# Two engines issue six blocks of a linear-attention and MLP kernel in the program's order, with smaller stages

## The chip, the cores and the metric

The kernel runs on one core of one Trainium2 chip. The metric is device time in microseconds (us). Three runs before the change took 1603.47, 1610.88 and 1611.52 us, median 1610.88. A profiled execution took 1603.45 us with a span of 1601.6 us from the first to the last instruction of the program, so 1.85 us lie around the span.

## The reference

```python
kv  = einsum('bhsd,bhse->bhde', k, v)        # 8 batches, 8 heads, 576 rows, 64 columns
out = einsum('bhsd,bhde->bhse', q, kv)
x   = out / sqrt(mean(out*out, -1) + 1e-6) * g_norm    # -> 4608 tokens x 512
h   = x @ w_in                               # 512 x 2048
g   = where(h >= 1, h, where(h <= -1, 0, (h + 1)**2 / 4))
x1  = g @ w_out                              # 2048 x 512
r   = maximum(x1 @ w_in2, 0)
out = (r * r) @ w_out2
```

The weights arrive as 64-bit floats, the rest as 32-bit floats.

## The kernel before

Every product of the two MLPs is made to single precision out of three fp32r matmuls: an operand is split into a high half (a cast, mostly on ScalarE) and a low half (a subtraction on VectorE), and high*high, high*low and low*high are added up in PSUM (`mm3`, L222). A weight is first narrowed from 64 bits (`narrow_w`, L250: one activation on ScalarE, L255, and two integer operations on VectorE, L257 and L258) and then split (`split_halves`, L168: cast and subtraction).

A *block* is 512 tokens through one MLP. `blocks` (L1001) lists seven plain blocks, those of batches 0 to 6 through the first MLP, that run one after the other. A block has 16 steps, one for each 128 columns of the hidden width; step `t` is one turn of the loop at L1098. A step has two halves. In the first half `h_stage` (L635) issues 12 matmuls into one of two PSUM banks (tag "h") and then a relu (ScalarE, L650), a square (ScalarE, L212) and a clamp that reads the bank again (VectorE, L652). In the second half `g_stage` splits the result (cast L204, subtraction L218) and `out_stage` issues the 12 matmuls of two steps earlier (`LAG = 2`) into four accumulators. After 16 steps the accumulators are copied out (L683 on VectorE, L685 on ScalarE) and stored.

Other work is hung into these halves by `hook(s, f, ...)` (L1004), where `s` counts half steps:

- Attention of batch `b` runs during block `b - 1`, four pairs of heads, one each 7 half steps (`attention`, L604). For a pair that starts at half step `s`: `kv_stage` and `t_stage` at `s` (the product of k and v, its copies `kvbd` at L462 and L463, the transpose of q at L522 and its split, L523 and L524), `o_stage` at `s + 2` and `s + 3`, `r_stage` at `s + 5` (the sum of squares, logarithm, exponential, a Newton step on VectorE, and the split of x).
- In block 0 the remaining 26 weight tiles of the first MLP are narrowed and split by `split_w` (L263), one each half step, three steps ahead of use. Loads of the raw weights are six steps ahead (L1012).
- In blocks 1 to 6 the weights of the later stages are prepared (L1026 to L1044): loads, narrowings, sums and splits, with stores from ScalarE's queue (`pay`, L162) to a scratch area in HBM.

After the plain blocks, five pairs of blocks go through a product with seven sub-products in place of eight (`in_phase`, `out_phase`), and a last plain block follows.

The order on each engine isn't that of this text: the framework's scheduler takes the instructions of each engine as they become ready by its own estimate of all durations, earlier ones of the program first, so an instruction can be put ahead of others that the program has earlier. The order it finds is then fixed; on the chip each engine follows it and waits where an operand isn't there.

Of the kernel before, what the change touches and what calls it, by code (L numbers as in the profile page):

```python
# [76 lines left out]
def linear_attention_rms_two_mlps(  # L77
# [19 lines left out]
    NF = DFF // P  # L97
    TB = 512
# [5 lines left out]
    AHEAD = 3  # L104
# [26 lines left out]
    LAST_B = B - 1  # L131
# [18 lines left out]
    def keep_halves(L, which, i, n, t):  # L150

        made = MADE[which][2 * n : 2 * n + 2]
        hs = slice(0, 2)
        if L == 1 and None in made and not (which == 1 and i + n * NH >= NF - TAIL):
            hs = slice(1, 2) if made[0] is None else slice(0, 1)
        owed.append(
            (wsd[L, which, i // 2][:, 2 * n + hs.start : 2 * n + hs.stop, i % 2], t[:, hs])
        )
# [3 lines left out]
    def pay(n):  # L162

        for dst, src in owed[:n]:
            nc.scalar.dma_start(dst, src)
        del owed[:n]

    def split_halves(t, src, hi, lo):  # L168

        src = src.rearrange("p (h f) -> p h f", h=2)  # L170
        copy(hi, t[:, :, 0, :], src)
        lo.tensor_tensor(t[:, :, 1, :], src, t[:, :, 0, :].bitcast(F32), ALU.subtract)  # L172
# [11 lines left out]
    engines = {"A": nc.scalar, "D": nc.vector, "P": nc.gpsimd}  # L184
# [6 lines left out]
    def engine(op, phase):  # L191
        return engines[next(turns[op][min(phase, 2)])]

    def scaled(e, dst, src, scale):
        if e is nc.scalar:
            e.activation(dst, src, AF.Copy, scale=scale)
        elif e is nc.vector:
            e.tensor_scalar_mul(dst, src, scale)
        else:
            e.tensor_scalar(dst, src, scale, 0.0, op0=ALU.mult, op1=ALU.add)  # L200

    def copy(e, dst, src):
        if e is nc.scalar:
            e.copy(dst, src)  # L204
        elif e is nc.vector:
            e.tensor_copy(dst, src)
        else:
            scaled(e, dst, src, 1.0)

    def square(e, dst, src):  # L210
        if e is nc.scalar:
            e.activation(dst, src, AF.Square)  # L212
        else:
            e.tensor_tensor(dst, src, src, ALU.mult)

    def split(t, src, op, phase):
        copy(engine(op + "_hi", phase), t[:, 0, :], src)
        engine(op + "_lo", phase).tensor_tensor(  # L218
            t[:, 1, :], src, t[:, 0, :].bitcast(F32), ALU.subtract
        )  # L220
# [26 lines left out]
    def d_tile(name, dtype=F32):  # L247
        return dt.tile([P, TB], dtype, tag=f"dt{next(d_tags)}", name=name)

    def narrow_w(L, f, which, phase):  # L250

        raw = w_raw.pop((L, f, which))
        low, high = raw[:, :, 0], raw[:, :, 1]
        as_float = high.bitcast(F32)
        nc.scalar.activation(as_float, as_float, AF.Prelu, scale=REBIAS, alpha=SIGN)  # L255
        t = d_tile(f"d{L}_{which}_{f}", I32)
        nc.vector.tensor_scalar(t, low, 29, None, op0=ALU.logical_shift_right)  # L257
        nc.vector.scalar_tensor_tensor(  # L258
            t, high, 3, t, op0=ALU.logical_shift_left, op1=ALU.bitwise_or
        )  # L260
        return t.bitcast(F32)

    def split_w(L, f, which):  # L263

        phase = int(f >= AHEAD)
        w = narrow_w(L, f, which, phase)
        dst = wi if which == 0 else wo
        t = wp.tile([P, 2, 2, H2], F32R, tag=f"w{which}_{f}", name=f"w{L}_{which}_{f}")
        split_halves(t, w, engine("w_hi", phase), engine("w_lo", phase))
        dst[L, f] = t  # L270
        if which == 1 and f >= NF - TAIL:
            keep_halves(L, which, f % NH, f // NH, t.bitcast(F32))
# [89 lines left out]
    xs = {}  # L362
# [4 lines left out]
    hl = {}  # L367
    og = {}
# [6 lines left out]
    def bank(b, name):  # L375

        pool, tag = next(banks) if b == 0 else (ps_t, "at")
        return pool.tile([P, TB], F32, tag=tag, name=name)
# [67 lines left out]
    def kv_stage(b, hp):  # L446
        kt, vt = kvm.pop((b, hp))
        r = kvr.pop((b, hp))
        ps = bank(b, f"pkv_{b}_{hp}")


        kv = ps[:, :P]
        for c in range(MR):
            nc.tensor.matmul(kv, kt[:, c], vt[:, :, c, :], start=c == 0, stop=False)
        nc.tensor.matmul(kv, r[0], r[1], start=False, stop=True)
        for j in range(2):
            s = slice(j * D, (j + 1) * D)
            if b == 0:
                copy(engine("kv_hi", b), kv0[s, hp, s], ps[s, s])
                continue  # L460
            t = kvbd[turn[b, hp] % len(kvbd)]
            copy(engine("kv_hi", b), t[s, 0, s], ps[s, s])  # L462
            nc.vector.tensor_tensor(t[s, 1, s], ps[s, s], t[s, 0, s].bitcast(F32), ALU.subtract)  # L463
# [54 lines left out]
    def t_stage(b, hp):  # L518
        work = [ap1.tile([P, S], F32, tag=f"wk{n}", name=f"wk{n}_{b}_{hp}") for n in range(2)]
        qT = ap1.tile([P, S], F32, tag="wk2", name=f"qf_{b}_{hp}")  # L520
        parts = [ap1.tile([P, S], F32R, tag=f"hl{n}", name=f"qT{n}_{b}_{hp}") for n in range(2)]
        nc.vector.transpose(qT, qs.pop((b, hp)))  # L522
        copy(engine("q_hi", b), parts[0], qT)  # L523
        engine("q_lo", b).tensor_tensor(parts[1], qT, parts[0].bitcast(F32), ALU.subtract)  # L524
        hl[b, hp] = (work, parts)
# [19 lines left out]
    def r_stage(b, hp):  # L545
        (y, o), _ = hl.pop((b, hp))
        s2 = og.pop((b, hp))
        ms = []
        for half in range(2):
            c = slice(half * U, (half + 1) * U)  # L550
            ps = bank(b, f"pr_{b}_{hp}_{half}")
            m = ps[:, :U]
            for n in range(2):
                nc.tensor.matmul(m, ones, s2[n][:, c], start=n == 0, stop=n == 1)
            nc.scalar.activation(y[:, c], m, AF.Ln, bias=lnb, scale=LN_SCALE)
            ms.append((c, m))
        nc.scalar.activation(y, y, AF.Exp, bias=expb, scale=-0.5)
        t = ap1.tile([P, S], F32, tag="wk2", name=f"t_{b}_{hp}")
        square(engine("y", b), t, y)
        for c, m in ms:  # L560
            newton(t[:, c], m)
        if b < LAST_B:
            norm(t, y, o)
            nc.gpsimd.tensor_copy(xrem[b][:, hp, :], t[:, TB:])
            split(xs[1, b][hp], t[:, :TB], "x", b)
            return
        xt = st.tile([P, TB], F32, tag="st", name=f"xt_{hp}")
        nc.vector.scalar_tensor_tensor(t, t, -3.0, y, op0=ALU.add, op1=ALU.mult)
        nc.vector.tensor_tensor(xt, o[:, :TB], t[:, :TB], ALU.mult)
        nc.vector.tensor_tensor(xrem[b][:, hp, :], o[:, TB:], t[:, TB:], ALU.mult)  # L570
        x_kept[hp] = xt

    x_kept = {}

# [29 lines left out]
    def attention(b, base, every, order):  # L604

        slots = []
        for j, hp in enumerate(order):
            s = base + every * j
            turn[b, hp] = len(turn)
            slots += [  # L610
                (max(0, s - 7), load_kv, b, hp),
                (max(0, s - 7), load_q, b, hp),
                (s, kv_stage, b, hp),
                (s, t_stage, b, hp),
                (s + 2, o_stage, b, hp, 0),
                (s + 3, o_stage, b, hp, 1),
            ]
            if j == 0:
                slots.append((s + 5, begin, b))
            slots.append((s + 5, r_stage, b, hp))  # L620
            if b == LAST_B:
                slots.append((s + 7, keep_x, b, hp))
        if b < LAST_B:
            slots.append((2 * NF * b, store_xrem, b))
        return slots
# [378 lines left out]
    def hook(s, f, *a):  # L1004
        hooks.setdefault((s // 2, s % 2), []).append((f, a))
# [8 lines left out]
            hook(2 * i + w, load_w, 1, i + 6, w)  # L1014
    for i in range(NF - AHEAD):
        for w in range(2):
            hook(2 * i + w, split_w, 1, i + AHEAD, w)
    for b in range(1, PLAIN):
        for f in range(NF - TAIL, NF):
            hook(2 * (b * NF + f - 1) + 1, load_tail, b, f)  # L1020
# [5 lines left out]
    for j in range(2 * NH):  # L1026
        which, i = j % 2, j // 2
# [43 lines left out]
    for j in range(2):  # L1071
        s = slice(j * D, (j + 1) * D)
# [22 lines left out]

    N1 = len(blocks) * NF
    step = lambda t: (*blocks[t // NF], t % NF)
    for t in range(N1):  # L1098
        h_stage(*step(t))
        n = len(owed)  # L1100
        for f, a in hooks.get((t, 0), []):
            f(*a)
        pay(n)
        n = len(owed)
        g_stage(*step(t))
        if t >= LAG:
            out_stage(*step(t - LAG))
        for f, a in hooks.get((t, 1), []):
            f(*a)
        pay(n)  # L1110

    late = []
    for n in range(NS):
# [16 lines left out]
    L, b = 2, NB - 1  # L1130
# [47 lines left out]
```

## Time and profile before

| | |
|---|---|
| median of three runs | 1610.88 us (1603.47 to 1611.52) |
| profiled execution, its span | 1603.45 us, 1601.6 us |
| TensorE busy | 1573.7 us, 98% of the span |
| VectorE, ScalarE, GpSimd busy | 1071.9, 943.7, 135.2 us |
| mean of the granted TensorE clock | 0.993 of full speed |
| moved by DMA | 355.55 MB, mean 222 GB/s |

Busy time of an engine is the time in which one of its instructions ran. What an idle stretch waited for is read from the views of waits, and in which stage it lies from the views of windows and of the order of time. In these, PE is TensorE, DVE is VectorE, ACT is ScalarE, SP is SyncE; a queue has a "q" behind its engine. L12 is line 12 of the kernel.

### The profile page before, as it was taken

Reading aid. Unit: us, or ns where it says so; the run is one execution under the profiler, and the core shown is the slowest. Engines: PE = TensorE matmul, PEld = TensorE weight load, DVE = VectorE, ACT = ScalarE, POOL = GpSimd, SP = SyncE. Lnnn points to the kernel's source line nnn. Section 1 sums busy time; section 2 is a strip of 40 time slices with the busy share of each in tenths; the row PEclk is TensorE's granted clock in tenths of the full one; section 3 lists DMA queues with packets and bytes.
Section 4 is the critical chain, followed back from the end, with each engine's and each line's share of the span. In section 5 each row is a group of like instructions: output and inputs, shape, how many; then the busy total and the mean of one; then the engine's idle time right before and its main releaser. Section 6 shows DMA issues by size and latency. Waiting matters only on the chain. (4 is left out here: it accounts for less than half of the span.)

```text
span 1601.6 us, 20867 instructions
## 1 busy us (share of the span) xinstructions
PE 1573.7 (98%) x7112; PEld 1295.6 (81%) x7112; DVE 1071.9 (67%) x1806; ACT 943.7 (59%) x1731; POOL 135.2 (8%) x117
## 2 busy tenths in 40 slices
PE   8999999999999999999999999999999999999998
PEld 5788888888878888788888888887788888888887
DVE  6887776877867787553487549776964496457522
ACT  5787666667666676664665466455646563664321
POOL 0000000000000000001310121012101300320000
PEclk9899999999999999999999999999999999999999
DMA  9897878796877978724676867696676677876783
GB/s 280 236 285 239 245 247 272 222 288 195 246 227 237 285 213 262 256 76 151 197 239 196 223 212 243 193 245 175 221 247 203 215 223 194 244 217 184 191 249 105
DMA packets 327513, 355.55 MB, mean 222 GB/s; under 512 B 196464, under 2 KB 221040, under 8 KB 327408
## 3 DMA queue, kind: packets, MB, share of 16 engines
q1 hardware_dynamic: 288496, 282.91, 61.7%
q10 hardware_dynamic: 38912, 71.31, 11.9%
q8 instruction: 57, 0.93, 0.2%
q14 instruction: 48, 0.39, 0.1%
HBM read 270.01 MB, written 84.15 MB: 221 GB/s over the span
## 5 line engine op out<-in xcount | busy, mean ns | idle before, releaser
L829 PE MATMUL po<-t,ws 128*128 128x512 f32 x1680 | 385.6, 391 | 3.3 <-DVE t L765 2.9
L829 PE MATMUL ph<-x,ws 128*128 128x512 f32 x1680 | 384.4, 391 | 2.3 <-DVE e L874 2.3
L829 PEld LDWEIGHTS po<-t,ws 128*128 128x128 f32 x1680 | 314.2, 188 | 74.0 <-DVE t L765 8.8
L829 PEld LDWEIGHTS ph<-x,ws 128*128 128x128 f32 x1680 | 316.4, 188 | 69.3 <-DVE e L874 3.6
L225 PE MATMUL ph<-x,w 128*128 128x512 f32 x1344 | 335.5, 394 | 5.8 <-ACT x L204 3.4
L225 PEld LDWEIGHTS ph<-x,w 128*128 128x128 f32 x1344 | 249.5, 189 | 58.1 <-ACT x L204 4.4
L765 DVE TENSOR_TENSOR t<-g,t 128x512 fp32r<-128x512 f32 x240 | 169.1, 710 | 80.6 <-ACT t L204 78.7
L204 ACT CAST t<-g 128x512 fp32r<-128x512 f32 x240 | 145.3, 621 | 89.5 <-DVE t L765 61.1
L225 PE MATMUL acc<-gs,w 128*128 128x512 f32 x696 | 172.6, 393 | 2.3 <-ACT ev L685 2.3
L225 PE MATMUL acc<-gs,wt 128*128 128x512 f32 x648 | 156.8, 391 | 0.0
L225 PEld LDWEIGHTS acc<-gs,w 128*128 128x128 f32 x696 | 128.7, 188 | 28.2 <-ACT ev L685 2.7
L225 PEld LDWEIGHTS acc<-gs,wt 128*128 128x128 f32 x648 | 120.4, 188 | 24.2
L650 ACT ACTIVATE u<-ph,halfb 128x512 f32<-128x512 f32 x112 | 77.1, 689 | 101.2 <-PE ph L225 100.2
L881 DVE TENSOR_TENSOR h<-ph,e 128x512 f32<-128x512 f32 x120 | 82.5, 690 | 61.8 <-PE ph L829 55.3
L652 DVE SCALAR_TENSOR_TENSOR u<-u,ph 128x512 f32<-128x512 f32 x112 | 76.5, 684 | 66.3 <-ACT u L212 65.5
L204 ACT CAST gs<-u 128x512 fp32r<-128x512 f32 x128 | 79.4, 621 | 57.0 <-DVE u L652 32.6
L895 POOL TENSOR_TENSOR t<-g 128x512 f32<-128x512 f32 x40 | 53.8, 1344 | 693.0 <-DVE h L881 284.3
L218 DVE TENSOR_TENSOR gs<-u,gs 128x512 fp32r<-128x512 f32 x128 | 87.8, 687 | 36.2 <-ACT gs L204 34.9
L888 ACT ACTIVATE h<-h 128x512 f32<-128x512 f32 x96 | 60.6, 631 | 57.3 <-DVE h L881 52.8
L874 DVE TENSOR_TENSOR e<-ph,e 128x512 f32<-128x512 f32 x80 | 54.1, 687 | 53.2 <-PE ph L829 52.3
L204 ACT CAST x<-xr 128x512 fp32r<-128x512 f32 x74 | 45.9, 621 | 49.4 <-DVE xr L797 35.1
L212 ACT ACTIVATE u<-u 128x512 f32<-128x512 f32 x112 | 70.6, 632 | 1.7 <-DVE s L172 1.1
(127 smaller groups left out, 1715.9 us busy)
## 6 DMA issues: line engine op xcount, KB each, us to landing
ws<-wsd SPq DMA_DIRECT2D x312, 512.0 KB, 4.0
wsd<-s ACTq DMA_DIRECT2D x96, 512.0 KB, 4.4
wt<-wsd SPq DMA_DIRECT2D x54, 512.0 KB, 4.9
raw<-in_moe_w_in_dram SPq DMA_DIRECT2D x32, 512.0 KB, 5.4
raw<-in_moe_w_out_dram SPq DMA_DIRECT2D x32, 512.0 KB, 5.3
xr<-x1d SPq DMA_DIRECT2D x36, 256.0 KB, 5.0
wsd<-w ACTq DMA_DIRECT2D x17, 512.0 KB, 4.6
k<-in_k_dram SPq DMA_DIRECT2D x32, 256.0 KB, 5.8
```

The costliest lines, as they stand in the source:

```text
L204: e.copy(dst, src)
L212: e.activation(dst, src, AF.Square)
L218: engine(op + "_lo", phase).tensor_tensor(t[:, 1, :], src, t[:, 0, :].bitcast(F32), ALU.subtract)
L225: nc.tensor.matmul(dst, wt(a), xt(c), start=first and n == 0, stop=last and n == 2)
L650: nc.scalar.activation(u, ps, AF.Relu, bias=halfb, scale=0.5)
L652: nc.vector.scalar_tensor_tensor(u, u, 1.0, ps, op0=ALU.min, op1=ALU.max)
L765: engine2(op + "_lo").tensor_tensor(t[:, 1, :], src, t[:, 0, :].bitcast(F32), ALU.subtract)
L829: nc.tensor.matmul(ps, wt(a), xt(c), start=first and n == 0 and i == 0, stop=last and n == len(lhs) - 1 and i == 2, skip_group_check=True,)
L874: nc.vector.tensor_tensor(e[i, p], bank, e[i, 1], ALU.add)
L881: nc.vector.tensor_tensor(h, bank, add, ALU.add)
L888: nc.scalar.activation(u, h, AF.Relu)
L895: engine2("t_sum").tensor_tensor(t1[k], b, a, ALU.subtract)
```

## The change

ScalarE (`Activation`) and VectorE (`DVE`) issue everything that the first 96 steps (blocks 0 to 5) emit in the order of the program. TensorE, GpSimd and SyncE stay with the scheduler, and so does where instructions emitted outside of the region fall among those inside. Block 6 and all that follows are as before.

Within the half steps, work is divided anew:

- The copies `kvbd` out of PSUM (`kv_copy`) and the split of q (`q_split`) come a half step after the product and the transpose.
- `r_stage` ends with the square at `s + 5`; the Newton step and the norm (`n_stage`) come at `s + 6`, the split of x (`x_stage`) at `s + 7`.
- `split_w` is divided: the narrowing stays at its half step, the split into halves comes one half step later. The six tiles made before step 0 are still done in one.

```diff
+    narrowed = {}
+
+    def first_half(L, f, which):
+        narrowed[L, f, which] = narrow_w(L, f, which, int(f >= AHEAD))
+
+    def second_half(L, f, which):
         phase = int(f >= AHEAD)
-        w = narrow_w(L, f, which, phase)
+        w = narrowed.pop((L, f, which))
         ...
@@ kv_stage
+        pkv[b, hp] = ps
+        if b == 0:
+            kv_copy(b, hp)
+
+    def kv_copy(b, hp):
+        ps = pkv.pop((b, hp))
         ...
@@ t_stage
         nc.vector.transpose(qT, qs.pop((b, hp)))
+        hl[b, hp] = (work, parts, qT)
+
+    def q_split(b, hp):
+        work, parts, qT = hl.pop((b, hp))
         copy(engine("q_hi", b), parts[0], qT)
         ...
@@ r_stage
         square(engine("y", b), t, y)
+        og[b, hp] = (y, o, t, ms)
+
+    def n_stage(b, hp):
+        y, o, t, ms = og[b, hp]
         for c, m in ms:
             newton(t[:, c], m)
         if b < LAST_B:
             norm(t, y, o)
             nc.gpsimd.tensor_copy(xrem[b][:, hp, :], t[:, TB:])
-            split(xs[1, b][hp], t[:, :TB], "x", b)
             return
         ...
+    def x_stage(b, hp):
+        t = og.pop((b, hp))[2]
+        if b < LAST_B:
+            split(xs[1, b][hp], t[:, :TB], "x", b)
@@ attention
                 (s, t_stage, b, hp),
+                (s + 1, kv_copy, b, hp),
+                (s + 1, q_split, b, hp),
                 ...
             slots.append((s + 5, r_stage, b, hp))
+            slots.append((s + 6, n_stage, b, hp))
+            slots.append((s + 7, x_stage, b, hp))
@@ hooks of block 0
-            hook(2 * i + w, split_w, 1, i + AHEAD, w)
+            hook(2 * i + w, first_half, 1, i + AHEAD, w)
+            hook(2 * i + w + 1, second_half, 1, i + AHEAD, w)
@@ main loop
-    for t in range(N1):
+    def one_step(t):
         h_stage(*step(t))
         ...
+    with tc.manual_schedule(engines={mybir.EngineType.Activation, mybir.EngineType.DVE}):
+        for t in range(N1 - NF):
+            one_step(t)
+    for t in range(N1 - NF, N1):
+        one_step(t)
```

## Rows read from the trace of the kernel before

**Rows 1.** The page: busy time by engine, and the granted clock in 40 slices.
```profile
PE 1573.7 (98%) x7112; PEld 1295.6 (81%) x7112; DVE 1071.9 (67%) x1806; ACT 943.7 (59%) x1731; POOL 135.2 (8%) x117
...
PEclk9899999999999999999999999999999999999999
```

**Rows 2.** Waits of TensorE, whole span: who waited for whom; us, times, longest.
```profile
PE ph L225 <- ACT x L204: 3.4, 2, 1.9
...
PE po L225 <- ACT qT L204: 2.8, 2, 2.0
...
PE acc L225 <- ACT ev L685: 2.3, 1, 2.3
...
PE ph L225 <- DVE x L218: 1.2, 1, 1.2
...
PE ph L225 <- DVE u L652: 1.1, 2, 0.8
PE po L225 <- ACT kvbd L204: 1.0, 1, 1.0
```

**Rows 3.** Windows of blocks 0 and 1: length, busy us (instructions) by engine, clock, DMA.
```profile
47.00:147.00 100.00, 98.93 (x467) 82.45 (x467) 86.57 (x159) 80.86 (x161) 1.88 (x4) 0.99 0.86 258
147.00:245.00 98.00, 98.00 (x469) 82.42 (x468) 74.00 (x139) 67.28 (x134) 1.81 (x4) 1.00 0.81 252
```

**Rows 4.** Order of time, VectorE then TensorE: start, us, what [idle before].
```profile
460.99 0.43 DVE L257 TENSOR_SCALAR d<-raw 128x512 int32<-128x512 int32 x1 [3.19 <-DMA raw<-in_moe_w_in_dram]
...
462.30 0.78 DVE L522 STREAM_TRANSPOSE qf<-q 128x576 f32<-128x576 f32 x1
...
463.84 0.40 PE L225 MATMUL po<-qT,kvbd 128*128 128x288 f32 x1 [2.04 <-ACT qT L204]
```

**Rows 5.** Waits of VectorE, 45 to 631 us.
```profile
DVE d L257 <- DMA raw<-in_moe_w_in_dram: 24.2, 10, 3.7
```

**Rows 6.** Order of time before step 0, ScalarE then VectorE.
```profile
40.61 0.62 ACT L204 CAST x<-t 128x512 fp32r<-128x512 f32 x1 [0.82 <-DVE t L494]
...
41.10 0.79 DVE L257 TENSOR_SCALAR d<-raw 128x512 int32<-128x512 int32 x2
41.81 1.28 DVE L258 SCALAR_TENSOR_TENSOR d<-raw,d 128x512 int32<-128x512 int32 x2
43.02 0.68 DVE L218 TENSOR_TENSOR x<-t,x 128x512 fp32r<-128x512 f32 x1
```

**Rows 7.** Groups of instructions: count | busy us, mean ns | idle before.
```profile
L650 ACT ACTIVATE u<-ph,halfb 128x512 f32<-128x512 f32 x112 | 77.1, 689 | 101.2 <-PE ph L225 100.2 <-DVE s L347 0.4
L652 DVE SCALAR_TENSOR_TENSOR u<-u,ph 128x512 f32<-128x512 f32 x112 | 76.5, 684 | 66.3 <-ACT u L212 65.5
L212 ACT ACTIVATE u<-u 128x512 f32<-128x512 f32 x112 | 70.6, 632 | 1.7 <-DVE s L172 1.1
...
L524 DVE TENSOR_TENSOR qT<-qf,qT 128x576 fp32r<-128x576 f32 x28 | 21.1, 752 | 2.0 <-ACT qT L204 2.0
...
L204 ACT CAST qT<-qf 128x576 fp32r<-128x576 f32 x28 | 18.8, 670 | 16.9 <-DVE qf L522 15.4 <-DMA wsd<-s 1.3
...
L463 DVE TENSOR_TENSOR kvbd<-pkv,kvbd 64x64 fp32r<-64x64 f32 x56 | 12.3, 219 | 9.2 <-ACT kvbd L204 8.0
```

**Rows 8.** Order of time, TensorE: 12 matmuls right behind those of `h_stage` of step 4.
```profile
63.81 2.89 PE L225 MATMUL acc<-gs,w 128*128 128x512 f32 x12
```

**Rows 9.** Order of time, SyncE's queue: a raw weight load.
```profile
61.29 0.37 SPq L237 DMA_DIRECT2D raw<-in_moe_w_in_dram  x1
```

**Rows 10.** DMA issues, 40 to 140 us: count, size, us to landing.
```profile
wsd<-w ACTq DMA_DIRECT2D x13, 512.0 KB, 4.1
raw<-in_moe_w_in_dram SPq DMA_DIRECT2D x12, 512.0 KB, 4.8
```

**Rows 11.** End of block 5: ScalarE in order of time, and a window.
```profile
646.55 0.58 ACT L685 COPY ev<-acc 128x512 f32<-128x512 f32 x1 [3.95 <-DMA x1d<-ev]
...
645.00:650.00 5.00, 2.81 (x8) 2.45 (x9) 0.69 (x1) 2.45 (x5) 0.00 (x0) 0.68 0.70 271
```

More of the change, by code (lines that the diff above doesn't have):

```diff
@@ L263, in split_w @@
     def split_w(L, f, which):
+        first_half(L, f, which)
+        second_half(L, f, which)
+    narrowed = {}
+    def first_half(L, f, which):
+        narrowed[L, f, which] = narrow_w(L, f, which, int(f >= AHEAD))
+    def second_half(L, f, which):
         phase = int(f >= AHEAD)
-        w = narrow_w(L, f, which, phase)
+        w = narrowed.pop((L, f, which))
         dst = wi if which == 0 else wo
@@ L455, in kv_stage @@
         nc.tensor.matmul(kv, r[0], r[1], start=False, stop=True)
+        pkv[b, hp] = ps
+        if b == 0:
+            kv_copy(b, hp)
+    pkv = {}
+    def kv_copy(b, hp):
+        ps = pkv.pop((b, hp))
         for j in range(2):
```

## Prediction

> **What bounds the kernel now.** I read the page first: TensorE is busy for 1573.7 of 1601.6 us, VectorE for 1071.9 and ScalarE for 943.7, and the granted clock is at nine tenths or more in every slice [rows 1]. So TensorE bounds it, and the change touches neither its instructions nor the work of another engine: it can win only what TensorE waits for, 27.9 us of idle time in the whole span and what the clock loses around it. The next view is that of TensorE's own waits, and the reader is to sort them by stage [rows 2]. The waits for x (3.4 from ScalarE, 1.2 from VectorE) lie before step 0. The 2.3 for an accumulator's copy lies at step 97, behind the region. Inside the region lie 2.8 for the split of q, 1.0 for the copies of the k-v product, and 1.1 for a clamp that frees a bank: 4.9 us in some 590. The windows say the same of whole blocks: block 0 leaves TensorE 1.07 us idle of 100, block 1 none of 98, while VectorE works 86.6 and 74.0 us in them, ScalarE 80.9 and 67.3 [rows 3]. There is little to win in the stage that changes, and both engines have room left.
>
> Why those few waits are there is read in order of time. At 460.99 VectorE starts a narrowing after 3.19 us of waiting for a raw weight to land; the transpose of q, at 462.30, stands behind it in the queue; the split of q follows, and TensorE waits 2.04 us for it at 463.84 [rows 4]. The narrowing was put ahead of attention by the scheduler because it reckoned the load to be there. VectorE waited so ten times, 24.2 us in all [rows 5].
>
> The Trainium skill ("TensorE: Matmul & The Clock Gate", section on the architectural detail of the array) says that the queues of ScalarE and VectorE are strictly first in, first out. The trace agrees in the rows just named: a ready transpose stood behind a load of 3.19 us. By that rule an order fixed by hand makes each wait hold all that the program has behind it, so it speaks against the change as much as for it; this is the slower rival below, priced there from rows.
>
> **The change part by part.**
>
> *Waits that go.* In the program's order a narrowing of the later weights comes five half steps behind its load, and the split of q one half step behind the transpose, so the pattern of rows 4 should not come up. The same holds for the copies of the k-v product, and for the clamp, which now stands right behind its square. I take all 4.9 us as gone; ends: none of it goes, 0, and all of it, -4.9. Late next is nothing that TensorE waits for in these places; the next limit is its own work.
>
> *The start.* The last part of x is cast by 40.61 + 0.62 = 41.2, but VectorE subtracts at 43.02, since two L257 and two L258 (0.79 + 1.28 = 2.07 us) run in between [rows 6]. The instructions of step 0 and later now wait behind the first relu, which needs x. Six tiles are made before step 0; I count seven narrowings begun by then, so one pair of the two is of a later tile: half of 2.07, -1.0. Ends: 0 (the scheduler puts another tile there) and -2.1. That tile's work comes back in block 0, where VectorE has 100 - 86.6 = 13 us free.
>
> *A step in order.* From the end of the 12 matmuls of `h_stage`: relu 0.69, square 0.63, clamp 0.68, 2.0 us in a row [rows 7]. TensorE wants that bank again after three groups of 12 matmuls, 3 x 2.89 = 8.7 us [rows 8]. So everything that stands in front of clamp or relu may be late by 6.7 us at no cost; beyond that TensorE pays all of it. The heaviest half step of block 0 has on VectorE the clamp 0.68, a narrowing (2.07 / 2 = 1.04), a tile's subtraction and the norm's two operations (all of the sizes of rows 7, 0.7 to 0.75), and two Newton steps of half width, an estimate of 0.45 each: 4.8 us against 2.89 of TensorE. It leaves 1.9 us of lateness, under 6.7. Cost 0; if the cover goes, 1.9 us for each of 24 pairs is the other end, and I hold it unlikely, since VectorE has 13 us free in a block and the next half steps are light.
>
> *The moved attention work.* Nothing is added: copies, splits and norms keep their instructions. But a half step's work on ScalarE and VectorE runs while TensorE is one half step ahead. In half of the pairs (12 of 24, those with an odd start) `kv_copy` and `q_split` fall into a first half, behind relu and square: 0.69 + 0.63, then two casts and two subtractions of 64x64 in turn (0.22 each, 0.9), then 0.67 and 0.75 for q, 3.6 us in all [rows 7]. TensorE reaches the product with q after one group, 2.89 [rows 8]: 0.7 late, at most 12 x 0.7 = 8.4 us if it stands there. At least 0: the scheduler still orders TensorE and can put the next 12 matmuls first. The nearest row is what TensorE waited for the same two things before, 2.8 + 1.0 us; I take +3.0. What is queued behind a late product is ScalarE's three evictions of it and the next relu, which have the 6.7 us. The Newton step, a half step later, holds the sum's bank longer; TensorE's product of the next pair needs it after a group of matmuls more, and is again the scheduler's to place. The other halves of moved steps (x, at `s + 7`) are needed a block later: 0.
>
> *Loads and stores.* A narrowing starts on ScalarE, so a late raw weight now holds ScalarE and VectorE together. Example in block 0: the load issued at 61.29 lands 4.8 us later, 66.1 [rows 9, 10]; step 4's matmuls end at 63.81, relu and square take it to 65.1, so ScalarE waits 1.0 us there [rows 7, 8]. Hidden in 6.7: 0. Ends: 0 and +24.2, all that VectorE waited on such loads before [rows 5]. SyncE's queue keeps its order by the scheduler, and its loads wait for earlier transfers to end. ScalarE's queue also issues the stores of halves. In 40 to 140 us it issues 13 whole ones, though block 0 has only nine tiles to store by the program; four came early [rows 10] and now go to their places in blocks 1 to 3. That takes 4 x 0.5 MB, about 8 us at 258 GB/s, out of a block where DMA is busy for 0.86, and puts it where it is 0.81 [rows 3]. Neither was on TensorE's path: 0, and if anything raw weights land earlier.
>
> *Behind the region.* At step 97 ScalarE waits 3.95 us to copy an accumulator, because the tile is still being stored; TensorE stops for 2.3, and the window at 645 to 650 shows a clock of 0.68, a stretch at 1.2 GHz in place of 2.4 [rows 2, 11]: 5 x 0.32 = 1.6 us more. Block 6 isn't in the region, so I leave it: 0, between -3.9 and +3.9 as transfers fall otherwise.
>
> *The sum.* 1603.45 - 4.9 - 1.0 + 3.0 = 1600.5 us, against the profiled execution. That execution stands at the lower of two levels of the runs (1603.5, and 1610.9 to 1611.5, 7.4 us up); the median is at the upper. I can't say at which the next median falls, 1600.5 or 1608, and predict 1604, between them.
>
> **The rivals.**
>
> *The stalls only move.* As many new waits come as go, 1603.5 (at the median's level 1611). For it: the old order had only 4.9 us of them, which is already what an order found by readiness can do. Against: the pattern of rows 4 has one cause, and the program's order takes it away.
>
> *Start and block 6 gain too.* All 4.9, the whole 2.1, and 3.9 at step 97 with no new waits: -10.9, 1592.5 (1600 at the median's level). For it: fewer stores in flight and less work pulled ahead. Against: nothing in the change orders step 97.
>
> *Loads at the head of both queues* (the other side). Where raw weights land late, the relu stands behind the narrowing on ScalarE and the clamp behind it on VectorE. It decides from the point at which a wait and the lateness at hand pass 6.7 us together: a load late by 4.8. If half of 24.2 us reaches TensorE, +12.1 on the sum, 1612.6 (1620 at the median's level). For it: SyncE's queue has little lead in block 0 [rows 9, 10] and ten such waits stood in the old order. Against: the longest of these waits was 3.7 [rows 5], and the narrowings now come later.
>
> **How the numbers follow.** The forecast (1600.5 at the profile's level) 0.45, stalls only move 0.12, start and block 6 gain 0.27 (with what the two levels of the runs give by chance), loads at the head 0.16. Over 0.5%, 8 us, is about what a measurement of this kernel can tell from no change: faster 0.27, within 0.57, slower 0.16. The range goes from 1591, just below the faster rival, to 1620, the slower one at the median's level.
>
> **What would show it.** In the profile after: TensorE's waits for the split of q, the copies and the clamp inside the first 630 us below 3 us in sum, and no wait of VectorE for raw weights in blocks 1 to 5; the subtraction of the last x a microsecond earlier behind its cast; VectorE's and ScalarE's busy time unchanged; 2.3 us at the copies of block 5's accumulators still there. Wrong would be: TensorE's waits above 10 us in the region, most of them on a clamp with ScalarE in front held by a load, or a gap long enough to bring a stretch at 1.2 GHz into blocks 1 to 5.

## The result, and the profile after

The changed kernel takes 1625.39 us (median of 4 runs, 1623.92 to 1625.85); the kernel before, run beside it, 1610.72 (1603.47 to 1611.52). The ratio is 1.010, 95% interval 1.007 to 1.0129: slower, with an interval clear of 1, and outside the range of 1591 to 1620. The profiled execution took 1625.6 us with a span of 1623.6, 22.0 us over the span before, where the medians differ by 14.7: the profiled execution of the kernel before was its fastest of four, and 22 executions of it beside later runs spread from 1601.05 us (mean granted clock 0.995) to 1616.00 (0.990). The 22.0 us below are those of this one pair of executions.

The page of the kernel after, busy time by engine and the granted clock in 40 slices:

```profile
PE 1581.6 (97%) x7111; PEld 1291.9 (80%) x7112; DVE 1080.7 (67%) x1806; ACT 950.5 (59%) x1731; POOL 138.3 (9%) x117
...
PEclk9899999999999999999999999999999999999999
```

Against [rows 1], ScalarE works 6.8 us more and VectorE 8.8 us more, both under 1%, so neither engine has become the bound. TensorE's idle time grew from 27.9 to 42.0 us, and its busy time by 7.9. What it waits for, whole span (who waited for whom; us, times, longest):

```profile
PE ph L225 <- DVE u L685: 13.1, 13, 1.8
PE ph L225 <- ACT x L204: 4.0, 2, 2.7
...
PE acc L225 <- ACT gs L204: 3.0, 1, 3.0
...
PE acc L225 <- DVE gs L218: 2.1, 2, 1.9
...
PE po L225 <- DVE qT L545: 0.3, 1, 0.3
```

The waits that the prediction set out to remove are gone: ScalarE's split of q and the copies of the k-v product, 3.8 us in [rows 2], are not in the list any more; the 0.3 for q's low half on VectorE stood before too. In their place stands the clamp (L685 after the change), 1.1 us before and 13.1 now. The windows of [rows 3] for the kernel after (length, busy us and instructions of TensorE, its weight loads, VectorE, ScalarE, GpSimd; clock, DMA share, GB/s):

```profile
47.00:147.00 100.00, 92.20 (x419) 73.15 (x419) 82.24 (x146) 76.33 (x149) 2.15 (x4) 0.98 0.76 230
147.00:245.00 98.00, 97.44 (x463) 81.26 (x462) 66.13 (x119) 64.35 (x126) 1.68 (x4) 1.00 0.69 210
```

Block 0's window holds 419 matmuls in place of 467. VectorE and ScalarE do less in it than before: they are late and idle at once. To place the loss I counted matmuls in the trace and compared when the last of the 12 matmuls of `out_stage` of a step ended. Microseconds by which a kernel is behind the one before, after step 0, block 0 (step 16), half of the region (48, 64), block 5's last steps (92), and the region (98). Each line is of one execution, and its kernel is told of below:

```
after step                          0     16     48     64     92     98
after                             1.6   10.3   17.7   20.0   16.5   23.5
order in blocks 1 to 5            0.0   -1.5    3.7    6.0    2.7    9.8
order in block 0                  2.1   16.7   18.2   18.8   16.8   13.7
order in blocks 0 to 4            2.0   11.0   17.4   19.7   25.8   21.9
casts first                       1.5    7.2   12.7   12.6    7.3   11.8
weights in four parts             1.7    9.2   14.2   16.5   13.6   20.1
both                              1.2    5.8   11.7   11.8    6.3    9.2
casts first, blocks 1 to 4        0.9   -0.5    6.4    6.3    4.0    1.7
less ScalarE work in block 0      3.2    7.7   13.4   15.7   13.1   19.9
less VectorE work in block 0      1.6    4.4   10.2   12.5    9.9   16.0
division alone, no order         -1.6   -2.9    3.5    5.1    3.4    2.5
division, casts first, no order   6.1    4.8    6.3    8.1    8.2    7.8
```

The last two lines are of kernels that are no slower by their medians, so a figure of the table can be off by several microseconds. It also holds what TensorE's own order moves: the scheduler puts a step's `out_stage` now earlier, now later among other work. By the products of `h_stage`, the kernel after is 2.8 us ahead after step 1, then 10.9 behind after step 16, 13.2 after 48, 16.3 after 64, 15.8 after 92 and 24.8 after 98. So it loses most, 13.7 us, in block 0; another 5.4 by step 64, nothing to 92, and 9.0 in steps 92 to 98. Now one stretch of block 0, all engines in order of time (start, us, what [idle before]):

```profile
72.29 2.92 PE L225 MATMUL acc<-gs,w 128*128 128x512 f32 x12
...
73.47 0.67 ACT L683 ACTIVATE u<-ph,halfb 128x512 f32<-128x512 f32 x1
73.62 0.78 DVE L539 STREAM_TRANSPOSE qf<-q 128x576 f32<-128x576 f32 x1
74.17 0.63 ACT L212 ACTIVATE u<-u 128x512 f32<-128x512 f32 x1
74.33 0.65 DVE L172 TENSOR_TENSOR w<-d,w 128x512 fp32r<-128x512 f32 x1
...
74.71 0.19 ACT L204 CAST kvbd<-pkv 64x64 fp32r<-64x64 f32 x1
74.90 0.41 DVE L257 TENSOR_SCALAR d<-raw 128x512 int32<-128x512 int32 x1
75.42 0.69 DVE L258 SCALAR_TENSOR_TENSOR d<-raw,d 128x512 int32<-128x512 int32 x1
76.03 0.68 DVE L685 SCALAR_TENSOR_TENSOR u<-u,ph 128x512 f32<-128x512 f32 x1
...
76.62 0.21 DVE L480 TENSOR_TENSOR kvbd<-pkv,kvbd 64x64 fp32r<-64x64 f32 x1
...
76.76 1.43 PE L225 MATMUL ph<-x,w 128*128 128x512 f32 x5 [1.55 <-DVE u L685]
76.86 0.21 ACT L204 CAST kvbd<-pkv 64x64 fp32r<-64x64 f32 x1 [1.97 <-DVE kvbd L480]
```

The reader is to follow three things. The square that the clamp reads ends at 74.80, yet the clamp starts at 76.03: VectorE has a transpose, a weight's low half and a narrowing ahead of it. TensorE is done at 75.21 and waits 1.55 us for that clamp. And ScalarE, after the first of its two casts of the k-v product, stands 1.97 us before the second: VectorE's first subtraction uses the same PSUM bank and the same tile `kvbd`, comes before the second cast in the program, and is itself behind the clamp. Until then neither the cast of q's high half nor any later relu can start. In this step ScalarE and VectorE each wait for what the other has queued.

ScalarE's waits in the region, 45 to 640 us, kernel after:

```profile
ACT kvbd L204 <- DVE kvbd L480: 41.5, 24, 3.5
ACT x L204 <- DVE t L511: 29.7, 21, 1.7
ACT s L558 <- PE po L225: 23.3, 12, 3.8
...
ACT u L683 <- PE ph L225: 3.7, 4, 1.4
```

and the same engine in the kernel before, 45 to 631 us:

```profile
ACT u L650 <- PE ph L225: 73.1, 58, 2.8
...
ACT kvbd L204 <- DVE kvbd L463: 2.9, 2, 2.5
```

Before, ScalarE stood ready for TensorE's next bank 58 times; after, 4 times. The wait between the two casts was 2.9 us in all before, and is 41.5 after. The relu of steps 2 to 5 started 0.0 to 1.1 us behind the end of its 12 matmuls before and 6.9 to 9.0 after; over steps 2 to 13 of block 0 it was 0.0 to 7.0 before and is 6.7 to 12.1 after. The Trainium skill ("PSUM — Partial Sum Buffer", section on terms, rows on the bank and the quadrant) says that two engines on the same bank and the same quadrant of 32 partitions at once are an error, and that different quadrants of a bank may be accessed at the same time. The two halves lie in partitions 0 to 63 and 64 to 127, so by that rule the second cast needn't wait for the first subtraction; the order that this framework gave made it wait 24 times, whether for the bank or for the tile `kvbd` that both write, and no run here tried the two at once.

### The profile page after: what moved, and what is told of

The parts are those of the page before. It is cut to its first block, busy times and chain, and to the rows that moved or that the text cites. A ratio compares the mean times of both kernels' runs of the same rounds, so it can differ in the third digit from the quotient of the medians.

```text
span 1623.6 us, 20967 instructions
## 1 busy us (share of the span) xinstructions
PE 1581.6 (97%) x7111; PEld 1291.9 (80%) x7112; DVE 1080.7 (67%) x1806; ACT 950.5 (59%) x1731; POOL 138.3 (9%) x117
## 5 line engine op out<-in xcount | busy, mean ns | idle before, releaser
L225 PE MATMUL ph<-x,w 128*128 128x512 f32 x1344 | 345.8, 398 | 17.5 <-DVE u L685 13.1
L225 PE MATMUL acc<-gs,wt 128*128 128x512 f32 x648 | 161.6, 393 | 4.9 <-ACT gs L204 3.0
L685 DVE SCALAR_TENSOR_TENSOR u<-u,ph 128x512 f32<-128x512 f32 x112 | 76.7, 685 | 56.6 <-ACT u L212 56.2
```

Source lines behind the costliest of these rows:

```text
L225: nc.tensor.matmul(dst, wt(a), xt(c), start=first and n == 0, stop=last and n == 2)
L685: nc.vector.scalar_tensor_tensor(u, u, 1.0, ps, op0=ALU.min, op1=ALU.max)
```

## The experiments

Theory 1: the order on both engines costs the 22 us, the division nothing. Rivals: the division does it; or one engine's order alone does.

**The division alone.**

```diff
-    with tc.manual_schedule(engines={mybir.EngineType.Activation, mybir.EngineType.DVE}):
-        for t in range(N1 - NF):
-            one_step(t)
-    for t in range(N1 - NF, N1):
+    for t in range(N1):
         one_step(t)
```

> The stages are divided as in the changed kernel, but the scheduler orders ScalarE and VectorE again. Theory 1 (the fixed order makes the two engines wait for each other at the heads of their queues, and the division is harmless): the 22 us of the profiled executions go, span 1598 to 1606 us, TensorE's waits for the clamp in block 0 under 2 us. Rival (the half-step-later hand-overs themselves make clamp and splits late): span 1615 us or more, with waits for the clamp in block 0 still 5 us or more.

1604.46 us, ratio 0.9987 (0.9963 to 1.001), and no wait of TensorE for the clamp is left in its profile. The division by itself costs nothing that can be told; the order does. The order of TensorE and SyncE stays with the scheduler, which makes it anew for every edit. No run separates what that does from what the two fixed queues do.

**The order alone** (the kernel before, its loop put under the same order).

```diff
+    with tc.manual_schedule(engines={mybir.EngineType.Activation, mybir.EngineType.DVE}):
+        for t in range(N1 - NF):
+            one_step(t)
```

> The kernel before, with only the fixed order of ScalarE and VectorE over blocks 0 to 5; copies, splits and norms stay in their old half steps. Theory 1: the hand-overs inside one half step now each cost a wait at a queue's head, so it is slower than the changed kernel: span 1630 us or more. Rival (the division costs, the order does not): at or under the kernel before, 1595 to 1605 us.

1670.67 us, ratio 1.04 (1.036 to 1.0441). Waits of TensorE, whole span, and of ScalarE, 45 to 190 us:

```profile
PE ph L225 <- DVE u L652: 38.7, 20, 5.3
PE acc L225 <- ACT gs L204: 8.3, 5, 3.6
```

```profile
ACT w L204 <- DVE d L258: 32.0, 26, 1.8
```

A tile narrowed and split in one go makes ScalarE wait for VectorE at each of the 26 tiles of block 0, 1.2 us each. So the division, of the weight tiles and of the attention work together, is worth about 45.6 us under this order (spans 1669.2 and 1623.6), and still leaves the order dearer than none.

**The order in blocks 1 to 5, and in block 0.**

```diff
+    for t in range(NF):
+        one_step(t)
     with tc.manual_schedule(engines={mybir.EngineType.Activation, mybir.EngineType.DVE}):
-        for t in range(N1 - NF):
+        for t in range(NF, N1 - NF):
```

> The changed kernel, with block 0 left to the scheduler and only blocks 1 to 5 in the program's order. Theory 1 with block 0 as its place (both engines carry 26 weight tiles there and have least room): the 10.3 us lost between steps 4 and 14 come back, span 1611 to 1615 us; the 7 us lost at steps 94 to 98 stay. Rival (late loads at the heads, blocks 1 to 5): span stays at 1620 us or more.

```diff
-        for t in range(N1 - NF):
+        for t in range(0, NF):
             one_step(t)
-    for t in range(N1 - NF, N1):
+    for t in range(NF, N1):
```

> The changed kernel, with only block 0 in the program's order. Theory 1: block 0 is 10 us longer than before and nothing is lost behind it, span 1609 to 1613 us. Rival (late loads in blocks 1 to 5 make most of the loss): span under 1606 us.

Blocks 1 to 5: 1614.03 us, 1.0056 (1.0035 to 1.0077). Block 0: 1618.24, 1.008 (1.0055 to 1.0105). The spans are 8.2 and 11.9 us over that of before, both just outside what was expected (1611 to 1615 and 1609 to 1613). Together that is 20.1, near the 22.0 of the whole, but the parts don't simply add: by the table the second loses 14.6 in block 0, where the kernel after loses 8.7. In it TensorE waits 3.3 us there for a load of v, 0.6 in the kernel after. The first loses little in four blocks (2.7 us at step 92) and 7.1 us in steps 92 to 98. So the loss has two main places, block 0 and the last steps of block 5.

**One engine's order.**

```diff
-    with tc.manual_schedule(engines={mybir.EngineType.Activation, mybir.EngineType.DVE}):
+    with tc.manual_schedule(engines={mybir.EngineType.Activation}):
```

> The changed kernel, with ScalarE alone held to the program's order; VectorE is the scheduler's again. Theory 1 (the two queues wait for each other, so it takes both orders): less than half of the 22 us is lost, span 1602 to 1611 us. Rival (one engine's order is what costs, ScalarE's, since relu, evictions and loads of raw weights stand in it): span 1616 us or more.

```diff
-    with tc.manual_schedule(engines={mybir.EngineType.Activation, mybir.EngineType.DVE}):
+    with tc.manual_schedule(engines={mybir.EngineType.DVE}):
```

> The changed kernel, with VectorE alone held to the program's order. Holding ScalarE alone cost 36 us of span, so theory 1 in its first form (it takes both orders) has fallen. Theory 2 (what costs is that relu and evictions, which TensorE waits for, stand in ScalarE's fixed queue behind casts that wait for VectorE): with ScalarE free, little is lost, span 1601 to 1608 us. Rival (either order costs, since the other engine's free order then runs ahead of it): 1615 us or more.

1639.34 us with ScalarE's order, 1632.24 with VectorE's (one run each, spans 35.7 and 28.7 us over that of before). Both theories fell here, that it takes the two orders and that ScalarE's alone does it. The second run's rival came true: either order costs, and more than both. VectorE in the first (45 to 640 us), then ScalarE in the second:

```profile
DVE d L257 <- DMA raw<-in_moe_w_in_dram: 34.8, 11, 6.6
```

```profile
ACT raw L255 <- DMA raw<-in_moe_w_out_dram: 15.9, 4, 7.7
ACT raw L255 <- DMA raw<-in_moe_w_in_dram: 12.6, 5, 5.6
```

The engine left free runs ahead by the scheduler's estimate and stands before a load, as in [rows 4], now with an engine behind it that may not go round it. That this is why one order costs more than two was only argued from these waits, not shown.

**Theory 2: hand-overs between the two queues.** Three edits to the changed kernel loosen them. *Casts first* issues both casts of the k-v product and then both subtractions; *weights in four parts* puts activation, integer operations, cast and subtraction of a weight tile of block 0 a half step apart each (`w_one` to `w_four`, whose definitions aren't shown); the third does both.

```diff
-        for j in range(2):
-            s = slice(j * D, (j + 1) * D)
+        halves_of = [slice(j * D, (j + 1) * D) for j in range(2)]
+        for s in halves_of:
             ...
-            nc.vector.tensor_tensor(t[s, 1, s], ps[s, s], t[s, 0, s].bitcast(F32), ALU.subtract)
+        for s in halves_of:
+            ...
+                nc.vector.tensor_tensor(t[s, 1, s], ps[s, s], t[s, 0, s].bitcast(F32), ALU.subtract)
```

> The changed kernel, with the copies of the k-v product in another order: the casts of both heads on ScalarE first, then both subtractions on VectorE; before, ScalarE's second cast stood behind VectorE's first subtraction (41.5 us of ScalarE's waits, 24 times). Theory 1: ScalarE's wait goes nearly whole, block 0 loses 5 to 8 us in place of 10, span 1613 to 1620 us. Rival (the load of VectorE alone sets block 0, so ScalarE's waits cost nothing): span 1622 to 1626 us.

```diff
-            hook(2 * i + w, first_half, 1, i + AHEAD, w)
-            hook(2 * i + w + 1, second_half, 1, i + AHEAD, w)
+            for n, part in enumerate((w_one, w_two, w_three, w_four)):
+                hook(2 * i + w + n, part, 1, i + AHEAD, w)
```

> The changed kernel, with each weight tile of block 0 in four parts a half step apart (activation, narrowing, cast, subtraction), where the narrowing and the split were one half step each; the work is the same. Theory 1: VectorE no longer waits at its head for a cast or activation of the same half step (24 us of ScalarE's and 16 us of VectorE's waits in 45 to 150 us), block 0 loses under 5 us, span 1612 to 1619 us. Rival (too much work for the two engines in block 0, whatever its order): as the changed kernel, 1622 to 1626 us.

> Casts first and loose weights together. Theory 1: block 0 as long as before (within 2 us), what is left are the late loads of blocks 1 to 5 and step 94 to 98: span 1609 to 1614 us. Rival (load of the engines): 1620 us or more.

Casts first: 1615.15 us, 1.0069 (1.0048 to 1.009), span 12.0 under that of the kernel after. Four parts: 1622.98, 1.0115 (1.0098 to 1.0132), span 3.3 under. Both: 1613.42, 1.005 (1.0034 to 1.0066), span 14.1 under. ScalarE's longest waits with casts first, 45 to 640 us:

```profile
ACT s L561 <- PE po L225: 31.6, 18, 4.3
ACT x L204 <- DVE t L514: 30.8, 22, 1.7
ACT gs L204 <- DVE u L688: 18.4, 32, 1.6
```

The 41.5 us behind the subtraction are gone, and the edit moves only the order of four instructions of 0.2 us a pair. So this one hand-over is a large piece of the loss. How large is less sure than the 12.0 us of one pair of executions: 3.4 of them are two stretches at 1.2 GHz, at 361.65 and 644.95, that the kernel after has and this one hasn't. The medians lie 10.2 us apart and the four runs of each don't overlap; against the kernel before beside each it is 14.7 and 10.8 us. Of the 12.0, 3.1 come back in block 0, the rest behind it (table). The next wait of this kind, x's cast behind the norm, stays at 30.8 us, and no run loosened it.

Four parts alone can't be told from the kernel after: the runs overlap (1621.46 to 1625.46), and 7.5 us are lost in block 0 where under 5 were expected. Still they show something. The relu of steps 2 to 13 is only 2.9 to 6.6 us late there, and TensorE's waits of block 0 move from the clamp to the split behind it (45 to 165 us):

```profile
PE acc L225 <- DVE gs L218: 3.7, 3, 1.3
PE ph L225 <- DVE u L714: 1.8, 1, 1.8
```

The runs of both edits together overlap with those of casts first. Its span lies in the expected 1609 to 1614, but block 0 loses 4.6 us, not the 2 that were expected at most.

**The region one block shorter.** Whether the loss of steps 92 to 98 belongs to the loads of that place or to the region's end.

```diff
-        for t in range(N1 - NF):
+        for t in range(0, N1 - 2 * NF):
             one_step(t)
-    for t in range(N1 - NF, N1):
+    for t in range(N1 - 2 * NF, N1):
```

> The changed kernel, with the region ending a block earlier: block 5 is the scheduler's. What the changed kernel lost around steps 94 to 98 followed a raw weight for which ScalarE waited 5.6 us at its queue's head. Theory (this wait at the head, and the late order behind it, are the cause): the 6 us go, span 1614 to 1619 us, no wait of TensorE over 2.5 us near step 94. Rival (the end of block 5 loses as much wherever the region ends, as it did 2.3 us before): 1621 us or more.

1626.85 us, 1.0123 (1.0094 to 1.0151). What I expected came true in one half: nothing is lost in steps 92 to 98 any more (25.8 to 21.9). But 6.1 us are lost between 64 and 92 (9.5 by the products of `h_stage`), and the time stayed. TensorE there, in order of time:

```profile
556.56 4.61 PE L225 MATMUL ph<-x,w 128*128 128x512 f32 x12 [3.24 <-DVE u L685]
616.84 0.40 PE L575 MATMUL pr<-s2lo,ones 128*128 128x288 f32 x1 [3.19 <-DVE s2lo L564]
```

For comparison, the kernel after at step 94:

```profile
643.10 0.65 ACT L255 ACTIVATE raw<-raw 128x512 f32<-128x512 f32 x1 [5.57 <-DMA raw<-in_moe_w_out_dram]
...
645.40 4.40 PE L225 MATMUL acc<-gs,wt 128*128 128x512 f32 x12 [2.97 <-ACT gs L204]
```

In the kernel after it is a raw weight, 5.57 us late at ScalarE's head, with 12 matmuls of 4.40 in place of 2.89 us behind the gap. Every kernel here with both orders in block 5 has such a wait at that place, 3.63 to 5.57 us, and by the products of `h_stage` loses 1.9 to 10.3 us in steps 92 to 98. With a shorter region it is other work: a clamp at step 81, just behind the region, and attention in block 5. The end of the region alone isn't the cause: the last run below, with casts first, ends its region at the same step and stands 3.4 us behind at step 80 and 3.6 at 92. Why this kernel loses more there was not tried further.

**The division and casts first, without any order; and the order where there is room** (blocks 1 to 4, casts first). The edits are those above, put together.

> No fixed order at all; the stages divided as in the changed kernel and the casts of both heads first. If the cast that waits for the other head's subtraction costs in the scheduler's order too (1.0 us of TensorE's waits stood on it before): 1 to 3 us under the kernel before, span 1599 to 1602 us. If the scheduler goes around it: no difference, 1602 to 1604.

> Casts of both heads first, and the program's order only in blocks 1 to 4, where both engines have room and no load was late. If the order costs nothing where there is room: span 1598 to 1602 us, within 0.5% of the kernel before, TensorE's waits inside blocks 1 to 4 under 2 us. If it costs there too: 1606 us or more.

1607.59 us, 1.0004 (0.9987 to 1.0021), and 1604.85, 0.9993 (0.9973 to 1.0013). Neither can be told from the kernel before. Their spans, 1608.3 and 1603.6, lie outside what was expected, and TensorE's waits inside blocks 1 to 4 are 3.9 us in the second, not under 2. In the second, TensorE's waits for the clamp in the whole span and block 0's window:

```profile
PE ph L225 <- DVE u L688: 1.9, 4, 0.9
```

```profile
47.00:147.00 100.00, 100.00 (x468) 83.26 (x468) 82.51 (x150) 77.64 (x155) 1.35 (x4) 0.98 0.74 217
```

Block 0, free to be ordered by readiness, leaves TensorE no idle time in this window, and the order in blocks 1 to 4 costs nothing that can be told. But it also wins nothing.

**Theory 3: in block 0 the two queues form one chain.** Which of them sets the loss? The next two leave out part of block 0's weight arithmetic, so their weights are other numbers.

```diff
-        nc.scalar.activation(as_float, as_float, AF.Prelu, scale=REBIAS, alpha=SIGN)
+        mlp1 = L == 1 and phase == 1
+        if not mlp1:
+            nc.scalar.activation(as_float, as_float, AF.Prelu, scale=REBIAS, alpha=SIGN)
         ...
-        nc.vector.scalar_tensor_tensor(
-            t, high, 3, t, op0=ALU.logical_shift_left, op1=ALU.bitwise_or
-        )
+        shift = ALU.logical_shift_right if mlp1 else ALU.logical_shift_left
+        nc.vector.scalar_tensor_tensor(t, high, 3, t, op0=shift, op1=ALU.bitwise_or)
```

> The changed kernel, but the 26 weight tiles of block 0 are narrowed without ScalarE's activation (the weights it makes are other numbers; only its time is read). 26 x 0.680 us = 17.7 us leave ScalarE in block 0, and VectorE keeps all its work. Theory 3 (in block 0 the two queues form one chain: ScalarE 81 us of work plus 24 us of waits for VectorE fill its time, and any time taken off either comes back to TensorE): block 0 loses at most 2 us in place of 10.3, in all 1612 to 1617 us. Rival (VectorE alone is late, by its own queue): block 0 still loses 8 us or more, 1622 to 1627.

```diff
+        if L == 1 and phase == 1:
+            nc.vector.scalar_tensor_tensor(
+                t, high, 3, high, op0=ALU.logical_shift_left, op1=ALU.bitwise_and
+            )
+            return t.bitcast(F32)
         nc.vector.tensor_scalar(t, low, 29, None, op0=ALU.logical_shift_right)
```

> The changed kernel, but the 26 weight tiles of block 0 are narrowed without VectorE's first integer operation, L257 (the weights it makes are other numbers; only its time is read). 26 x 0.423 us = 11.0 us leave VectorE in block 0, and ScalarE keeps all its work. Theory 3 (two queues as one chain): ScalarE's 24 us of waits for VectorE shrink by some 5 to 10, and block 0 loses 0 to 4 us in place of 10.3, in all 1613 to 1620 us. Rival (ScalarE alone is late by its own work and order): block 0 still loses 8 us or more, 1622 to 1627.

1621.6 us, 1.0086 (1.0058 to 1.0114), and 1618.35, 1.0061 (1.0038 to 1.0085). Their windows of block 0, first with less on ScalarE, then with less on VectorE:

```profile
47.00:147.00 100.00, 94.20 (x435) 76.51 (x435) 83.79 (x149) 65.48 (x128) 2.15 (x4) 0.97 0.78 234
```

```profile
47.00:147.00 100.00, 96.69 (x449) 78.66 (x450) 75.33 (x125) 80.36 (x156) 2.15 (x4) 0.98 0.77 231
```

From step 0 to 16 they lose 4.5 and 2.8 us, where the kernel after loses 8.7. So 17.7 us off ScalarE give back 4.2, and 11.0 us off VectorE 5.9. These are figures of one execution each; the ratios, 1.0086 and 1.0061 against 1.010, have intervals that overlap with that of the kernel after. With less on VectorE what was expected came true (0 to 4 us in block 0, 1613 to 1620 in all); with less on ScalarE it didn't (at most 2 us, 1612 to 1617). In the traces each engine's relief helps, so theory 3 is right in that, and too high in its size. With ScalarE idle for 34.5 us of 100, TensorE still waits for the clamp. That VectorE's queue counts for more is suggested by this, not shown. The amount of work alone doesn't make the loss: where block 0 has all of it and the scheduler's order, TensorE isn't idle (window above). It takes the fixed order and a load that leaves the order little room.

## Why the prediction was wrong

*What bounds the kernel: right.* TensorE bounds it still, and the other engines' busy time is nearly what it was. One reading of [rows 1] was off: the granted clock is at eight tenths in the second slice, not at nine in all; nothing in the sum used it.

*Waits that go: right for what it named first.* ScalarE's split of q and the copies, 3.8 us, are gone, and VectorE no longer waits for raw weights in the region, 24.2 us in [rows 5]. In their place it waits for ScalarE's activation of them, 5.7 us before (45 to 640 us):

```profile
DVE d L258 <- ACT raw L255: 23.1, 10, 4.4
```

The step called 4.9 us the gain, the clamp's 1.1 among them, and asked what is late next. The answer "nothing but its own work" was wrong, since the clamp's wait grew to 13.1.

*The start: right in its direction, mis-sized.* A microsecond earlier was forecast, 2.1 at most. The last products of steps 0 and 1 end at 43.0, 2.8 us earlier, and the subtraction of the last x starts 0.82 us behind the start of its cast, where it was 2.41 ([rows 6]). Before, then after (ScalarE, VectorE, TensorE):

```profile
43.75 2.08 PE L225 MATMUL ph<-x,w 128*128 128x512 f32 x4 [1.24 <-DVE x L218]
```

```profile
39.39 0.62 ACT L204 CAST x<-t 128x512 fp32r<-128x512 f32 x1
...
40.21 0.68 DVE L218 TENSOR_TENSOR x<-t,x 128x512 fp32r<-128x512 f32 x1
...
40.95 2.07 PE L225 MATMUL ph<-x,w 128*128 128x512 f32 x4 [0.16 <-DVE x L218]
```

In the kernels without an order in block 0 these products also end earlier than before, by 0.1 to 3.1 us, so that the order did it isn't shown. By the end of step 2 the gain is gone.

*A step in order: this step failed.* It left "1.9 us of lateness, under 6.7. Cost 0". It added the durations of VectorE's instructions in the heaviest half step and took the relu to start when the matmuls end. But the relu stands behind ScalarE's narrowing, casts and copies, and some of these wait for VectorE; VectorE's clamp stands behind work that waits for ScalarE in turn. The lateness is carried from one half step to the next: 6.7 to 12.1 us for the relu in steps 2 to 13, where the cover for the whole chain was 6.7. It begins with the relu of step 1, 10.4 us behind its matmuls (0.0 before): at 48.72 ScalarE has waited 3.35 us for the first product of k and v, and at 48.73 VectorE 4.01 for a load of q, both in front of it in the program. From there on everything keeps its place behind the late relu as long as block 0's weight tiles last; at step 16 the relu is on time again. The cover itself held up: with the lateness at or above it, TensorE waits for the clamp 7 times in the first 165 us, 9.1 us in sum (the first, 1.75 us at 44.78, before the relu of step 1), and in the other steps the matmuls of attention lie in between. The step's other end, 1.9 us for each of 24 pairs, 45.6 us, would have been the side to look at; 22.0 is half of it, but by another mechanism, so that is no credit to the estimate.

*The moved attention work: wrong in its cause.* It gave `kv_copy` 0.9 us by its four durations "in turn" and took +3.0 in all, for TensorE's waits for q's split and the copies; those waits are gone. What costs is the turn itself: each time ScalarE waits 1.7 us (41.5 over 24, up to 3.5) between two casts of 0.2. A row that hinted at it stood before: VectorE's subtraction `kvbd` L463 in [rows 7] waits 8.0 us for ScalarE's cast. Undoing the turn gave 10.2 us back by the medians, 12.0 by the profiled executions.

*Loads and stores, and the region's end: half right.* In block 0 no raw weight is late, but the first load of q that block 0 uses is, and holds VectorE's head for 4.01 us (order of time, VectorE, kernel after):

```profile
48.73 0.78 DVE L539 STREAM_TRANSPOSE qf<-q 128x576 f32<-128x576 f32 x1 [4.01 <-DMA q<-in_q_dram]
```

It stands where the lateness begins; what it costs by itself was not tried. One late raw weight at ScalarE's head, 5.57 us at step 94, past the decision point of 4.8 that the rival "loads at the head of both queues" named, did: 2.97 us of TensorE, and its next 12 matmuls took 1.5 us longer. That rival had the right sign and one of two places; its 1612.6 had the wrong mechanism for the larger part. "Behind the region" (0, up to 3.9) held: the 2.3 us at block 5's accumulators in [rows 2] are 0.7 us on VectorE's copy now, though they were to be still there as a sign.

*The signs of being wrong* came up in part. TensorE waits 14.7 us in 45 to 640 us, above the 10 that were named, 11.5 of them for the clamp; but ScalarE in front is held by VectorE's subtraction, not by a load. And a stretch at 1.2 GHz stands in block 3, at 361.65.

*The two levels of the runs*, 7.4 us apart, were no help either way: the medians differ by 14.7 us and the profiled executions by 22.2. Nor are they levels: the 22 later executions of the kernel before fill the range between and on both sides.

What is not settled: why an order on one engine alone costs more than on both; why TensorE's busy time, not only its idle time, grew by 7.9 us; how the loss divides between the two fixed queues and the scheduler's new order of TensorE and SyncE; and what is left in the kernel of both edits, 7.9 us of span over before. There TensorE waits 3.0 us for the split and 1.8 for the clamp in block 0, and 4.3 us are lost in steps 92 to 98 by the products of `h_stage`.

## What to carry to other kernels

Before fixing the issue order of two engines that hand work to each other, write down for each half step both queues in order and where one waits for the other; a sum of one engine's durations against the cover tells nothing when the other's queue stands in between. Alternate hand-overs (cast, subtract, cast, subtract on one buffer) are the first to undo, because each waits for all that the other engine has queued in front. In this kernel the fixed order cost nothing that can be told in blocks 1 to 4 with casts first, where VectorE and ScalarE are 73 to 76% and 65 to 69% busy before, and most in block 0, where they are 87% and 81% busy. And where an order found by readiness has left only 5 us of waits, that is nearly all that another can win.

## What the runs showed of the hardware

A gap of 1.03 us before the matmul at 361.53 in the kernel after was followed by a stretch at half clock (1.2 in place of 2.4 GHz) from 361.65 to 365.06, while the 2.04 us of [rows 4] in the kernel before were followed by none: rows in order of time, kernel after.

```profile
361.53 0.71 PE L225 MATMUL ph<-x,w 128*128 128x512 f32 x1 [1.03 <-DVE u L685]
...
362.28 3.07 PE L225 MATMUL ph<-x,w 128*128 128x512 f32 x7
365.19 1.99 PE L225 MATMUL acc<-gs,w 128*128 128x512 f32 x8
```

Seven matmuls take 3.07 us in that stretch and eight take 1.99 behind it. The same gap of 1.03 us, with one of 0.26 in front of it in all three, stands in the two kernels with less work in block 0, at 358.61 and 355.43, and no stretch at half clock follows there. The length of the gap alone doesn't tell.
